# Changing banks between two halves of a matmul group: a drain of TensorE against a semaphore of its own matmuls

## The chip, the cores and the metric

One core of one Trainium2 chip runs one program. The metric is the device time of one execution in microseconds (us), 2326.66 before the change (median of 3 runs, 2324.75 to 2327.2).

## What is computed

The reference mixes two branches of the same input with a gate per token. One branch is softmax attention with 32 heads of width 18, the other a layer norm with a two-layer MLP (576 to 4608 to 576, GELU between). There are 2048 tokens.

```
x = A_x                                                   # [1, 2048, 576]
g = sigmoid((x * gate_w).sum(-1, keepdims=True))
q, k, v = (x @ wqkv) split into 32 heads of width 18
a = softmax(q @ k.T * 18 ** -0.5) @ v, heads joined, @ wo
h = gelu(layernorm(x) @ w1 + b1)                          # 4608 wide
b = h @ w2 + b2
out = g * a + (1 - g) * b
```

All in float32. A product that has to be exact is made of three matmuls in a faster rounded format: each operand is split into a high and a low part, and high x high, high x low and low x high are summed in PSUM.

## The kernel before, in words

A first part (to about 250 us) projects queries, keys and values. Then one long loop does the attention and the MLP together. Its order of instructions is written out by the program: no scheduler moves anything, so what stands first in an engine's queue runs first.

**The loop.** There are 32 units (a pair of heads and half of the queries) of 16 steps, 512 steps in all; a step takes one chunk of 128 keys. The kernel finds the maxima of the scores ahead of their use, since softmax needs them before the exponentials.

- A **round** (`s1_round`, lines 192 to 204; `next_round`, 307) belongs to a unit two ahead. It makes two matmuls (L202, one for each head of the pair; one sits on rows 0 to 63 of TensorE's array and the other on rows 64 to 127, so that they run side by side), each into its own bank of PSUM from the pool `ps_s1`, which has three. VectorE reduces each bank to its maxima (L204). There are 32 rounds to a unit, two to a step.
- The **scores** of the second pass (`s2`, 243) are two matmuls side by side again (L251) into one double bank `pss`. There is only one of these: ScalarE's exponential (L253) of the scores before must have emptied it.
- `pv` (257) multiplies the exponentials of two chunks with the values (L268).
- Between these the loop calls `fill` (1222), which takes the next piece of the MLP from a generator (`mlp`, 315): the first layer of a pair of hidden chunks (`h_pair`, 465, matmuls L489, GELU on ScalarE and GpSimd), or the second layer for 128 tokens (`out_pair`, 583).

In the loop (1260 to 1282) `next_round()` stands ahead of the scores of the first half of a step and ahead of or behind those of the second half. The round, the scores and a piece of the MLP follow each other so.

**`out_pair`.** This is where the change is. It sums four hidden chunks of 128 rows into 128 tokens x 576 outputs: two banks of 288 columns each. Each product contracts over only 64 rows, so two matmuls run side by side, one on the upper and one on the lower half of the array. Two matmuls that run at the same time must not write to one bank. So there are two **turns** (L598): in the first, rows 0 to 63 sum into bank 0 and rows 64 to 127 into bank 1; in the second it is the other way round (`nn = h ^ turn`). Each turn has 12 steps (`k`), of one pair of matmuls each. Between the turns the last matmuls on one half must have ended before the other half writes into their bank, and that is what L603 is for:

```
            for turn in range(2):
                if turn == 1 and bare:
                    add(ps, g == 0)
                    ps = [psum(free_pool()) for _ in range(2)]
                elif turn == 1:
                    nc.tensor.drain()
```

`drain` holds TensorE's sequencer until all matmuls before it have ended. (`bare` is the end of the loop, when no rounds are left: there the turns use different banks, and nothing waits.) After the second turn VectorE adds both banks to the accumulator in SBUF (L593).

A piece of the MLP ends where `k` is in `ends`, a set that depends on the place in the step. Where an `out_pair` begins in the first place it is {7, 15}: the first piece holds steps 0 to 6, the second 7 to 14 with the change of turns at 12 in it, the third the rest. Behind a piece come the round and the scores of the loop. So in the program before, the instructions on TensorE around a change of turns are: round, scores, five pairs of the first turn, drain, three pairs of the second turn, round, scores.

The lines that matter here are L202, L204, L251, L253, L593, L603 and L614 (the output matmuls) of the kernel before. In the changed kernel the output matmuls are L630.

Of the kernel before, what the change touches and what calls it, by code (L numbers as in the profile page):

```python
# [28 lines left out]
G = 4  # L29
NFC = F // P  # L30
NG = NFC // G
ND = 288
# [26 lines left out]
def gated_mix_kernel(ctx: ExitStack, tc: tile.TileContext, x, wqkv, wo, w1, b1, w2, b2, gate_w, out):  # L59
    nc = tc.nc  # L60
# [38 lines left out]
    def psum(pool):  # L99
        return pool.tile([P, TB], F32, name="ps")  # L100
# [18 lines left out]
    def defer(n, fn):  # L119
        later.append((slot[0] + n, fn))  # L120
# [49 lines left out]
    def load_q(u):  # L170
        pair, half = unit(u)
        qa = QA[u % 3]
        for h in range(2):
            d0 = (2 * pair + h) * DH
            for i, part in enumerate((0, 0, 1)):
                r = 64 * h + i * DH
                dma_r(nc.sync, qa[r:r + DH, :], qk_scr[part, d0:d0 + DH, half * HALF:(half + 1) * HALF])

    def load_k(pair, c0=0, c1=S):
        ka = KA[pair % 3]  # L180
        for h in range(2):
            d0 = D + (2 * pair + h) * DH
            for i, part in enumerate((0, 1, 0)):
                r = 64 * h + i * DH
                dma_r(nc.sync, ka[r:r + DH, c0:c1], qk_scr[part, d0:d0 + DH, c0:c1])
# [6 lines left out]
    def s1_round(u, r):  # L192


        t, kb = (r % 8, r // 8) if u == 0 else divmod(r, 4)
        if r == 0:
            M4[u] = asm.tile([P, 2, 8, 4], F32, name="m4")
        qa, ka = QA[u % 3], KA[UNITS[u][0] % 3]
        for h in range(2):
            r0 = 64 * h  # L200
            ps = psum(ps_s1)
            nc.tensor.matmul(ps, qa[r0:r0 + 54, t * P:(t + 1) * P], ka[r0:r0 + 54, kb * TB:(kb + 1) * TB],  # L202
                             start=True, stop=True)
            nc.vector.tensor_reduce(M4[u][:, h, t, kb:kb + 1], ps, axis=AX.X, op=ALU.max)  # L204

    def s1_finish(u):

        m4 = M4.pop(u)
        nm = asm.tile([P, 2, 8], F32, name="nm")
        nm2 = asm.tile([P, 2, 2, 8], F32, name="nm2")  # L210
        nmh = asm.tile([P, 2, 8], F32R, name="nmh")
        nc.vector.tensor_reduce(nm, m4, axis=AX.X, op=ALU.max, negate=True)
        nc.vector.tensor_copy(nmh, nm)
        nc.vector.tensor_copy(nm2[:, :, 0, :], nmh.bitcast(F32))
        nc.vector.tensor_tensor(nm2[:, :, 1, :], nm, nmh.bitcast(F32), op=ALU.subtract)

        def rows():
            ps = psum(ps_s1)
            nc.tensor.transpose(ps[:32, :P], nm2.rearrange("p a b c -> p (a b c)"), ident)
            mr = asm.tile([32, P], F32R, name="mr", bufs=1)  # L220
            nc.scalar.activation(mr, ps[:32, :P], AF.Copy)
            qa = QA[u % 3]
            aside = slot[0] < ybusy[0]

            def store(h, b):
                r = 64 * h + 54 + b
                k = (h * 2 + b) * 8
                dma_r(nc.scalar if aside else nc.sync,
                      qa[r:r + 1, :].rearrange("o (t n) -> o t n", n=P), mr[k:k + 8, :].bitcast(F32))
            for k in range(4):  # L230
                if aside:
                    defer(1 + 2 * k, lambda k=k: store(*divmod(k, 2)))
                else:
                    store(*divmod(k, 2))
        if looped[0]:
            ROWS.append(rows)
        else:
            defer(8, rows)
# [62 lines left out]
    rounds = [(u, r) for u in range(NU) for r in range(NR)]  # L301
# [5 lines left out]
    def next_round():  # L307
        if rounds:
            u, r = rounds.pop()
            s1_round(u, r)  # L310
            if r == NR - 1:
                defer(1, lambda: s1_finish(u))


    def mlp():
        W1, W2, HT = {}, {}, {}
        RAW = {}
# [88 lines left out]
        def ready(table, key):  # L406
            while key not in table:
                bg.pop(0)[1]()
            return table[key]
# [35 lines left out]
        def cuts(n, pieces):  # L445

            return {(k * n + pieces - 1) // pieces for k in range(1, pieces)}
# [3 lines left out]
        def free_pool():  # L451

            if rounds:
                return ps_w
            turns[0] += 1
            return (ps_s1, ps_w)[(turns[0] - 1) // 2 % 2]
# [126 lines left out]
        def out_pair(i, t, acc):  # L583

            tb, g = seq[i]
            tok = slice(t * P, (t + 1) * P)
            cs = [slice(nn * ND, (nn + 1) * ND) for nn in range(2)]
            bare = not rounds

            def add(ps, base):  # L590
                for nn in range(2):
                    dst = acc[:, t, cs[nn]]
                    nc.vector.scalar_tensor_tensor(dst, ps[nn][:, :ND], 0.5, b2b[:, cs[nn]] if base else dst,  # L593
                                                   op0=ALU.mult, op1=ALU.add)
            ps = [psum(free_pool()) for _ in range(2)]
            ends = {7, 15} if piece[0] == 0 else cuts(24, (3, 2, 1)[piece[0]])
            k = 0
            for turn in range(2):  # L598
                if turn == 1 and bare:
                    add(ps, g == 0)  # L600
                    ps = [psum(free_pool()) for _ in range(2)]
                elif turn == 1:
                    nc.tensor.drain()  # L603
                for j in ORDER:
                    while (i, j) not in HT:
                        cut[0] = 3
                        yield 0
                    hh, hl = HT[i, j]
                    w_ = ready(W2, (i * (G // 2) + j // 2, j % 2))
                    for h_, p_ in ((hh, 0), (hh, 1), (hl, 0)):  # L610
                        for h in (0, 1) if turn == 0 else (1, 0):
                            r = slice(64 * h, 64 * h + 64)
                            nn = h ^ turn
                            nc.tensor.matmul(ps[nn][:, :ND], h_[r, tok], w_[p_][r, cs[nn]],  # L614
                                             start=(k == 0 or bare and k == 3 * G), stop=(k == 6 * G - 1 or bare and k == 3 * G - 1))
                        k += 1
                        if k < 6 * G:
                            if k in ends:
                                cut[0] = 1
                            yield 131  # L620
            add(ps, g == 0 and not bare)
            if g == NG - 1:
                tt = TBS[tb] * 4 + t
                nc.gpsimd.tensor_scalar(acc[:, t, :], acc[:, t, :], gate1[:, tt:tt + 1], 1.0, op0=ALU.mult, op1=ALU.mult)
                defer(12 if tb < NB - 1 else 4, lambda: nc.sync.dma_start(b_scr[tt * P:(tt + 1) * P, :], acc[:, t, :]))
            cut[0] = 2
            yield 131
# [69 lines left out]
    made = []  # L697
    W = {}
    stream = [mlp()]
    spent = [0.0]  # L700
    cut = [0]
# [43 lines left out]
    with ExitStack() as a:  # L745
# [215 lines left out]
        for tb in range(NB):  # L961
# [3 lines left out]
            for g, (fn, args) in enumerate(work):  # L965
# [49 lines left out]
                if tb == 2 and g == 13:  # L1015
                    ps = psum(ps_s1)
# [18 lines left out]
    RING.append(ring2)  # L1035


    def out_proj():

        OT, BT, done, tmp = {}, {}, {}, {}  # L1040
# [123 lines left out]
        for b in range(NB):  # L1164
            per = 4 if b == 2 else 1
            res = {}
            for i0 in range(0, 8, per):
# [3 lines left out]
                ps = {}  # L1171
                for cut_ in (range(4), range(4, 5)):
                    for t, n in tiles:
                        tok = slice(t * P, (t + 1) * P)
                        cs = slice(n * ND, (n + 1) * ND)
# [3 lines left out]
                        for c in cut_:  # L1179
# [3 lines left out]
                            for k, (s_, w_) in enumerate(prods):  # L1183
                                nc.tensor.matmul(ps[t, n][:, :ND], OT[b][3][:, s_, tok], w_part(w_, c)[:, cs],  # L1184
                                                 start=(c == 0 and k == 0), stop=(c == 4 and k == 1))
# [60 lines left out]
    for u in range(NU):  # L1246
        for kc in range(NT):
            step = u * NT + kc
            if kc == 1:
                if u + 2 < NU:  # L1250
                    load_q(u + 2)
                if u % 2 == 0 and u // 2 + 1 < NPAIR - 1:
                    load_k(u // 2 + 1)
                    load_v(u // 2 + 1)
                elif u == NU - 5:
                    load_k(NPAIR - 1)
                elif u == NU - 4:
                    load_v(NPAIR - 1)
            at[0] = step

            next_round()
            s2(u, kc, 0)
            run_due(462.0)
            if kc % 2:
                fill(step, 1)
            elif step > 0:
                pv(step - 2)
                while ROWS:
                    ROWS.pop(0)()
                run_due(2080.0)  # L1270
                if step <= 2 * LEAD:
                    next_round()
            else:
                fill(step, 2)
            if kc % 2:
                next_round()
            s2(u, kc, 1)
            if kc % 2 == 0:

                next_round()  # L1280
            run_due(462.0)
            fill(step, 2 if kc % 2 else 0)
    pv(NSTEP - 2)
# [28 lines left out]
```

## Time and profile before

| | |
|---|---|
| median of 3 runs | 2326.66 us |
| the profiled execution | 2327.55 us |
| its span, first to last instruction | 2325.8 us |
| mean granted clock of TensorE | 0.997 |
| TensorE busy / weight loads / VectorE / ScalarE / GpSimd | 99% / 69% / 72% / 59% / 41% |
| output matmuls on L614, each | 6,912 in all, 293 to 300 ns |
| rounds: matmuls on L202 | 2,048, 410 ns each, two at a time |
| maxima on L204 | 2,048, 684 ns each |
| exponentials on L253 | 1,024, 1,026 ns each |

The profile has one row for each group of instructions or each stretch of time. PE is TensorE's matmuls, PEld its weight loads (each matmul here has its own, and it runs beside the matmul before), DVE is VectorE, ACT ScalarE, POOL GpSimd. A tile that is written stands left of the arrow, those that are read right of it. "64*128" means 64 rows and 128 columns of the array. "idle before" is the time in which the engine did nothing ahead of the instruction, and the name behind the arrow is what ended it; "issue" is idle time which ended with nothing that the profile shows. Matmuls are pipelined and their ends are modelled: a pair side by side shows as two overlapping rows, and two starts a little over 0.13 us apart are two pairs at full pace.

### The profile page before, as it was taken

To read this page: it belongs to the slowest core of one execution; us is meant where nothing else is said; L and a number is where in the kernel's file an instruction comes from. 1 tells how busy PE (TensorE), PEld (TensorE's weight loads), DVE (VectorE), ACT (ScalarE), POOL (GpSimd) and SP (SyncE) were. 2 spreads that over 40 slices of the span, in tenths; PEclk is the share of its full clock that TensorE was granted. 3 is DMA by queue.
4 is the path that set the end of the run, shared out by engine and by line. 5 is a ranking of instruction groups with operands and counts; after the bars stand their busy time and mean duration, and the time that the engine had idled before them with its cause. 6 is when DMAs were issued, how large, how long until landed. Compare 5 with 4: busy or idle time off the path is not lost.

```text
span 2325.8 us, 50689 instructions
## 1 busy us (share of the span) xinstructions
PE 2295.2 (99%) x20601; PEld 1615.4 (69%) x20601; DVE 1663.7 (72%) x2921; ACT 1379.9 (59%) x1631; POOL 947.8 (41%) x936
## 2 busy tenths in 40 slices
PE   8999999999999999999999999999999999999999
PEld 7878666666666666666666666666666666666669
DVE  5675777777777777777777777777777777777545
ACT  4223666666666666666666666666666666666662
POOL 4002466566553434443444344434434443333320
PEclk9999899999999999999999999999999999999999
DMA  7756545445473524232263324233364233322346
GB/s 242 247 190 197 175 144 170 157 136 169 139 187 131 164 86 127 96 118 96 90 174 144 114 94 134 81 118 116 118 162 153 94 118 107 106 97 101 113 139 223
DMA packets 160654, 323.58 MB, mean 139 GB/s; under 512 B 56062, under 2 KB 83618, under 8 KB 149586
## 3 DMA queue, kind: packets, MB, share of 16 engines
q1 hardware_dynamic: 156582, 313.57, 43.1%
q10 hardware_dynamic: 3840, 6.78, 0.8%
q8 instruction: 162, 2.65, 0.5%
q14 instruction: 70, 0.57, 0.1%
HBM read 229.07 MB, written 95.16 MB: 139 GB/s over the span
## 4 chain that ended last, share of the span: by engine, by line
PE 90%; POOL 3%; DVE 2%; issue 2%; DMA 1%; ACT 1%; SPq 0%; ACTq 0%; POOLq 0%; DVEq 0%
PE ps L614 20%; PE ps L268 19%; PE ps L489 17%; PE pss L251 12%; PE ps L202 11%; PE ps L880 4%; PE ps L1184 3%; PE ps L898 2%; POOL zz L159 1%; POOL w L159 1%; POOL hl L159 1%; DVE m L204 1%; DMA wraw<-in_B_w_dram 1%; PE ps L795 0%; DMA p<-in_A_wqkv_dram 0%
## 5 line engine op out<-in xcount | busy, mean ns | idle before, releaser
L204 DVE TENSOR_REDUCE m<-ps 128x1 f32<-128x512 f32 x2048 | 1297.3, 684 | 431.2 <-PE ps L202 429.7
L253 ACT ACTIVATE p<-pss 128x1024 f32<-128x1024 f32 x684 | 701.7, 1026 | 456.9 <-PE pss L251 445.3
L489 PE MATMUL ps<-big,w 64*128 64x512 f32 x3834 | 514.8, 392 | 0.1
L614 PE MATMUL ps<-w,hh 64*128 64x288 f32 x4352 | 501.2, 300 | 13.8 <-ACT z L512 2.1
L159 POOL TENSOR_SCALAR zz<-zz 128x512 f32<-128x512 f32 x272 | 169.3, 622 | 827.4 <-ACT zz L575 761.8
L251 PE MATMUL pss<-qa,ka 56*128 56x512 f32 x2048 | 484.1, 437 | 3.8 <-ACT p L253 1.1
L253 ACT ACTIVATE ring<-pss 128x1024 f32<-128x1024 f32 x340 | 348.9, 1026 | 231.4 <-PE pss L251 225.6
L202 PE MATMUL ps<-ka,qa 54*128 54x512 f32 x2048 | 460.8, 410 | 2.8 <-DVE m L204 1.2
L614 PEld LDWEIGHTS ps<-w,hh 64*128 64x128 f32 x4352 | 402.4, 186 | 68.9 <-issue 42.4
L489 PEld LDWEIGHTS ps<-big,w 64*128 64x128 f32 x3834 | 390.1, 185 | 59.6 <-ACT vt L909 0.3
L159 POOL TENSOR_TENSOR zz<-zz,z 128x512 f32<-128x512 f32 x280 | 361.4, 1291 | 35.6 <-ACT zz L577 10.5
L251 PEld LDWEIGHTS pss<-qa,ka 56*128 56x128 f32 x2048 | 198.0, 185 | 254.6 <-ACT p L253 121.4
L614 PE MATMUL ps<-w,hl 64*128 64x288 f32 x2176 | 351.7, 293 | 0.0
L268 PE MATMUL ps<-p,vt 128*32 128x512 f32 x2736 | 344.5, 598 | 0.0
L202 PEld LDWEIGHTS ps<-ka,qa 54*128 54x128 f32 x2048 | 244.5, 185 | 34.0 <-DVE m L204 12.1
L614 PEld LDWEIGHTS ps<-w,hl 64*128 64x128 f32 x2176 | 236.2, 186 | 0.5
L159 POOL TENSOR_TENSOR w<-x,w 128x576 fp32r<-128x576 f32 (+1 forms) x34 | 68.3, 2012 | 308.8 <-ACT w L385 304.6
L159 POOL TENSOR_TENSOR hl<-zz,hh 128x512 fp32r<-128x512 f32 x134 | 174.1, 1300 | 19.0 <-ACT hh L538 8.1
L268 PE MATMUL ps<-ring,vt 128*32 128x512 f32 x1360 | 179.1, 598 | 0.0
L268 PEld LDWEIGHTS ps<-p,vt 128*32 128x32 f32 x2736 | 71.4, 109 | 147.3 <-issue 147.3
L593 DVE SCALAR_TENSOR_TENSOR x<-ps,x 128x288 f32<-128x288 f32 x270 | 110.8, 452 | 29.8 <-PE ps L614 16.4
L880 PE MATMUL ps<-big,wqk 128*128 128x512 f32 x504 | 123.4, 399 | 0.1
(122 smaller groups left out, 1403.3 us busy)
## 6 DMA issues: line engine op xcount, KB each, us to landing
w<-w_scr SPq DMA_DIRECT2D x54, 1152.0 KB
w<-w_scr SPq DMA_DIRECT2D x108, 576.0 KB
w_scr<-w SPq DMA_DIRECT2D x18, 1152.0 KB
w_scr<-w SPq DMA_DIRECT2D x36, 576.0 KB
qa<-qk_scr SPq DMA_DIRECT2D x192, 72.0 KB
ka<-qk_scr SPq DMA_DIRECT2D x90, 144.0 KB
x<-in_B_w_dram SPq DMA_DIRECT2D x34, 288.0 KB
qk_scr<-hh SPq DMA_DIRECT2D x36, 256.0 KB
```

The lines of the kernel that those rows point to most:

```text
L159: fn(*args, **kw)
L202: nc.tensor.matmul(ps, qa[r0:r0 + 54, t * P:(t + 1) * P], ka[r0:r0 + 54, kb * TB:(kb + 1) * TB], start=True, stop=True)
L204: nc.vector.tensor_reduce(M4[u][:, h, t, kb:kb + 1], ps, axis=AX.X, op=ALU.max)
L251: nc.tensor.matmul(ps[:, h, :], ka[r0:r0 + 56, kc * P:(kc + 1) * P], qa[r0:r0 + 56, qb * TB:(qb + 1) * TB], start=True, stop=True)
L253: nc.scalar.activation(RING[n % 3][:, qb], ps, AF.Exp, scale=SCALE)
L268: nc.tensor.matmul(OB[u][r:r + 32, :], v[:, k, 19 * h:19 * h + 32], RING[c % 3][:, qb, h, :], start=(k == 0), stop=(k == NT - 1))
L489: nc.tensor.matmul(ps[h], wt[w_][r, c, :], Y[s_][r, c, :], start=(k == 0), stop=(k == 26))
L593: nc.vector.scalar_tensor_tensor(dst, ps[nn][:, :ND], 0.5, b2b[:, cs[nn]] if base else dst, op0=ALU.mult, op1=ALU.add)
L614: nc.tensor.matmul(ps[nn][:, :ND], h_[r, tok], w_[p_][r, cs[nn]], start=(k == 0 or bare and k == 3 * G), stop=(k == 6 * G - 1 or bare and ...
L880: nc.tensor.matmul(ps, w_[:, c, ms], big[:, s_, :], start=(k == 0), stop=(k == len(prods) - 1))
L898: nc.tensor.matmul(ps[:, :ND], big[:, s_, tok], w_[:, c, cs], start=(k == 0), stop=False)
L1184: nc.tensor.matmul(ps[t, n][:, :ND], OT[b][3][:, s_, tok], w_part(w_, c)[:, cs], start=(c == 0 and k == 0), stop=(c == 4 and k == 1))
```

## The change

The drain between the turns becomes a wait on a semaphore, `turn_sem`, which the last matmul of the first turn on each half raises by one when it ends. The first matmul of the second turn waits until it has risen by two more. Two calls tell the framework that this wait takes the place of its own tracking; they put no instruction anywhere.

In front of the wait the generator issues one round of maxima's scores (`lend_round`), if rounds are left and no piece ends just there. The loop leaves out the next round that it would have issued itself (`loop_round`), so that their number stays.

```
+    lent = [0]
+
+    def lend_round():
+        if rounds and not lent[0]:
+            next_round()
+            lent[0] = 1
+
+    def loop_round():
+        if lent[0]:
+            lent[0] = 0
+        else:
+            next_round()
...
                 elif turn == 1:
-                    nc.tensor.drain()
+                    if 3 * G not in ends:
+                        lend_round()
+                    turned[0] += 2
+                    nc.tensor.wait_ge(turn_sem, turned[0])
...
-                            nc.tensor.matmul(ps[nn][:, :ND], h_[r, tok], w_[p_][r, cs[nn]],
-                                             start=(k == 0 or bare and k == 3 * G), stop=(k == 6 * G - 1 or bare and k == 3 * G - 1))
+                            mm = nc.tensor.matmul(ps[nn][:, :ND], h_[r, tok], w_[p_][r, cs[nn]],
+                                                  start=(k == 0 or bare and k == 3 * G), stop=(k == 6 * G - 1 or bare and k == 3 * G - 1))
+                            if bare:
+                                continue
+                            if k == 3 * G - 1:
+                                mm.then_inc(turn_sem, 1)
+                                tc.no_tile_sem_insts.add(mm.ins.name)
+                                tc.add_to_no_dep_group(f"turn{turned[0]}", mm.ins)
+                            elif k == 3 * G and h == 0:
+                                tc.declare_fence(mm.ins, group=f"turn{turned[0] - 2}")
...
+    turn_sem = tc.alloc_semaphore("turn")
+    turned = [0]
...
-            next_round()
+            loop_round()
             s2(u, kc, 0)
...
             if kc % 2:
-                next_round()
+                loop_round()
             s2(u, kc, 1)
             if kc % 2 == 0:
 
-                next_round()
+                loop_round()
```

What this does to the order shows on TensorE. Here are its instructions around one change of turns in the middle of the loop (the weights' tiles w_12473, w_12471, w_12467 are the hidden chunks in the order in which a turn takes them; a turn ends with w_12471 and begins with w_12467; the drain itself is not among the rows). Before:

```order
L614 MATMUL ps<-w_12473,hl 128x288 x2
L614 MATMUL ps<-w_12471,hh 128x288 x4
L614 MATMUL ps<-w_12471,hl 128x288 x2
L614 MATMUL ps<-w_12467,hh 128x288 x4
L614 MATMUL ps<-w_12467,hl 128x288 x2
L202 MATMUL ps<-ka_106,qa_104 128x512 [waits DVE_49] x2
L251 MATMUL pss<-qa_105,ka_108 128x512 [waits Activation_49]
```

The second turn begins at the row of w_12467,hh, three pairs ahead of the round. The same place in the changed kernel:

```order
L630 MATMUL ps<-w_12473,hl 128x288 x2
L630 MATMUL ps<-w_12471,hh 128x288 x4
L630 MATMUL ps<-w_12471,hl 128x288 x2
L202 MATMUL ps<-ka_106,qa_104 128x512 [waits DVE_49] x2
L630 MATMUL ps<-w_12467,hh 128x288 [waits turn]
L630 MATMUL ps<-w_12467,hh 128x288 x3
L630 MATMUL ps<-w_12467,hl 128x288 x2
L251 MATMUL pss<-qa_105,ka_108 128x512 [waits Activation_49]
```

The round has moved up by three pairs, to between the turns, and the first matmul behind it waits for the new semaphore. This occurs at all 137 changes of turns that had a drain; the other 7 of the 144 are the bare ones. The order on VectorE, ScalarE, GpSimd and the DMA queues is the same as before.

## The prediction

> **What bounds the kernel now.** I read the page first (busy shares, chain), then the list of waits, then the line of the drain by itself, and last the timeline of one stretch of 6 us in which the place that the change touches occurs once. From the page, the busy shares and the chain by engine:
>
> ```profile
> PE 2295.2 (99%) x20601; PEld 1615.4 (69%) x20601; DVE 1663.7 (72%) x2921; ACT 1379.9 (59%) x1631; POOL 947.8 (41%) x936
> PEclk9999899999999999999999999999999999999999
> PE 90%; POOL 3%; DVE 2%; issue 2%; DMA 1%; ACT 1%; SPq 0%; ACTq 0%; POOLq 0%; DVEq 0%
> ```
>
> TensorE carries 90% of the chain, at the full granted clock. Its 99% busy is modelled, so small holes are not in it; they show as idle time of the weight loads (PEld). The drain's own row (count; least, median, greatest ns), and from the list of waits (total us, times, longest us):
>
> ```profile
> L603 PEldq DRAIN  x137: 875/1188/1912, 256.3 to 2191.0; - x137
> ...
> PEld pss L251 <- ACT p L253: 121.4, 229, 1.4
> PEld pss L251 <- ACT ring L253: 62.4, 117, 1.0
> PEld ps L614 <- issue: 42.4, 137, 0.4
> PEld ps L202 <- DVE m L204: 12.1, 26, 0.8
> ```
>
> There are 137 drains, and 137 times the weight load of an output matmul follows idle time that no other engine ended: 42.4 / 137 = 0.31 us each. The drain's 1.2 us is no measure of the cost: the loads idle for 0.31 of it, so the sequencer reaches it early, with matmuls still queued. The row of L251 on L253 matters later: scores of the second pass wait 346 times for the exponential that empties their only bank.
>
> Now one site (start, length, engine, line; x counts instructions merged):
>
> ```profile
> 1013.54 0.19 PEld L251 LDWEIGHTS pss<-qa,ka 56*128 56x128 f32 x2 [0.84 <-ACT p L253]
> 1014.14 1.03 ACT L253 ACTIVATE p<-pss 128x1024 f32<-128x1024 f32 x1 [1.26 <-PE pss L251]
> 1014.30 2.48 DVE L204 TENSOR_REDUCE m<-ps 128x1 f32<-128x512 f32 x4 [0.99 <-PE ps L202]
> 1014.37 0.29 PE L614 MATMUL ps<-w,hl 64*128 64x288 f32 x2
> 1014.51 0.42 PE L614 MATMUL ps<-w,hh 64*128 64x288 f32 x4
> 1014.77 0.29 PE L614 MATMUL ps<-w,hl 64*128 64x288 f32 x2
> 1015.87 1.03 ACT L253 ACTIVATE ring<-pss 128x1024 f32<-128x1024 f32 x1 [0.71 <-PE pss L251]
> 1016.09 0.35 PE L614 MATMUL ps<-w,hl 64*128 64x288 f32 x2
> 1016.51 0.30 PEld L614 LDWEIGHTS ps<-w,hh 64*128 64x128 f32 x4 [0.31 <-issue]
> 1016.52 0.53 PE L614 MATMUL ps<-w,hh 64*128 64x288 f32 x4
> 1016.88 0.29 PE L614 MATMUL ps<-w,hl 64*128 64x288 f32 x2
> 1017.02 0.40 PE L202 MATMUL ps<-ka,qa 54*128 54x512 f32 x2
> 1017.25 0.40 PE L251 MATMUL pss<-qa,ka 56*128 56x512 f32 x2
> 1017.78 1.03 ACT L253 ACTIVATE ring<-pss 128x1024 f32<-128x1024 f32 x1 [0.88 <-PE pss L251]
> 1018.55 0.30 PE L614 MATMUL ps<-w,hl 64*128 64x288 f32 x2
> 1018.68 0.41 PE L202 MATMUL ps<-ka,qa 54*128 54x512 f32 x2
> 1018.86 0.26 PEld L251 LDWEIGHTS pss<-qa,ka 56*128 56x128 f32 x2
> 1018.87 0.82 DVE L593 SCALAR_TENSOR_TENSOR x<-ps,x 128x288 f32<-128x288 f32 x2
> 1018.92 0.51 PE L251 MATMUL pss<-qa,ka 56*128 56x512 f32 x2
> 1019.53 1.02 ACT L253 ACTIVATE p<-pss 128x1024 f32<-128x1024 f32 x1 [0.72 <-PE pss L251]
> ```
>
> The pair at 1016.09 is the last before the change of banks, the load at 1016.51 the first behind the drain. The round of maxima's scores that the change moves stands at 1017.02; the s2 scores at 1017.25 follow it.
>
> **1. The drain goes.** From the end of the pair before it (1016.09 + 0.35 = 1016.44) to the end of the third pair behind it (1016.88 + 0.29 = 1017.17) it takes 0.73 us; the same three pairs without a stop, from the pair at 1014.37 to that at 1014.77, take 0.40. The stop costs 0.33 us a site, near the 0.31 of the list, and 137 x 0.33 = 45 us over the run. All of it is on TensorE's path.
>
> **2. The wait comes.** No row shows TensorE waiting for itself, so I put it together. VectorE, waiting for the last output pair (1018.55, ending 1018.85), starts its add at 1018.87: 0.02 us behind the modelled end, its own start included. TensorE, waiting for ScalarE's exponential (1017.78 + 1.03 = 1018.81), starts its weight load at 1018.86: 0.05 behind. Together 0.05 to 0.07: the first load of the second turn would start at 1016.49 to 1016.51, where it starts now. So the wait **alone** gains 0 to 0.02 us a site, next to nothing: it lasts as long as the drain, since both wait for the same two matmuls. From above I bound it by a wait that ends only when the lent round has ended too: that round starts 0.13 behind the pair at 1016.09 (pairs follow so at 1014.37 and 1014.51), at 1016.22, ends by the model 0.40 later at 1016.62, and a load 0.07 behind that is 0.18 later than now. I take the lower end, since the load at 1018.86 starts while the round of 1018.68 is still in flight: a wait in front of a load does not wait for other matmuls. Queued behind the waiting load are all of TensorE's later instructions, hence also ScalarE's next exponential and VectorE's next maxima.
>
> **3. The round moves up by three pairs of matmuls, into the hole.** It takes TensorE 0.23 to 0.24 us where it stands (1017.02 to 1017.25, 1018.68 to 1018.92). In the new place it runs from 1016.22 to 1016.45 and the array waits for the load at 1016.49 to 1016.51 anyway, so it costs nothing there. Its cover is the stop; without that it would cost the same 0.23. The order of instructions has 137 such moves, none by more than three pairs, and one round less at the next regular place each time. TensorE's own gain: 0.23 for the round and 0 to 0.02 for the wait, 0.24 a site, 137 x 0.24 = 33 us.
>
> **4. What the round needs.** A bank out of three, which VectorE empties. VectorE's four reductions from 1014.30 take 0.62 each; the moved round's first matmul needs the second (1015.54, long done), its second matmul the third, done at 1016.16. With 0.05 to the load it loads at 1016.21 rather than at once, and ends about 0.1 + 0.23 later, at 1016.54. The first matmul of the second turn on that half of the rows starts 0.1 behind its load (the 0.53 of the four at 1016.52 against 0.42 of the four at 1014.51), at 1016.60. So this wait is hidden too, by about 0.06 us. VectorE gets the round's scores 0.80 us earlier (1016.22 for 1017.02); its order does not change, nor that of ScalarE, GpSimd or the queues.
>
> **5. What is late next: ScalarE.** By TensorE alone the s2 scores would start at 1017.25 - 0.24 = 1017.01. They need the bank that the exponential of 1015.87 leaves at 1016.90. Today the next exponential starts 0.88 behind that. How short can this be? In the two places where the load waited for the exponential, it starts 0.05 behind (1018.81 to 1018.86), and the next exponential 0.60 (1013.54 to 1014.14) to 0.67 (1018.86 to 1019.53) behind the load: 0.65 to 0.72 in all. So the exponential can move up by 0.16 to 0.23, and not by 0.24: ScalarE takes back 0.01 to 0.08 of TensorE's gain. A site with another spacing agrees:
>
> ```profile
> 1399.02 1.03 ACT L253 ACTIVATE p<-pss 128x1024 f32<-128x1024 f32 x1 [0.72 <-PE pss L251]
> 1399.23 0.41 PE L614 MATMUL ps<-w,hl 64*128 64x288 f32 x2
> 1399.72 0.30 PEld L614 LDWEIGHTS ps<-w,hh 64*128 64x128 f32 x4 [0.31 <-issue]
> 1400.46 0.40 PE L251 MATMUL pss<-qa,ka 56*128 56x512 f32 x2
> 1400.90 1.03 ACT L253 ACTIVATE p<-pss 128x1024 f32<-128x1024 f32 x1 [0.34 <-PE pss L251]
> ```
>
> There the exponential ends at 1400.05 and the next starts 0.85 behind: room for 0.13 to 0.20. Over both sites 0.13 to 0.23; I take 0.20, since the loads at a site follow a fresh start of both halves, as the one with 0.60 does. Everything later in the cycle (the waiting s2 load of 1018.86 too) hangs on this exponential and moves with it.
>
> **The sum.** 137 x 0.20 = 27 us (18 to 32 by the ends). The profiled execution took 2327.55 us, its span of 2325.8 and 1.75 around it; it lies 0.9 us above the median of the runs, 2326.66. From the median: 2299.5. Measurement can tell about 0.2%, 4.7 us, from no change.
>
> **The rivals.**
> *ScalarE does not hold it back* (0.11): where the later s2 scores have slack, TensorE's 0.24 counts in full: 33 us, 2293.5. For it: only 346 of the loads for 684 + 340 exponentials are listed as waiting.
>
> ```profile
> L253 ACT ACTIVATE p<-pss 128x1024 f32<-128x1024 f32 x684 | 701.7, 1026 | 456.9 <-PE pss L251 445.3
> L253 ACT ACTIVATE ring<-pss 128x1024 f32<-128x1024 f32 x340 | 348.9, 1026 | 231.4 <-PE pss L251 225.6
> ```
>
> Against: the two sites above.
> *The wait ends later than the drain did* (0.15). Both matmuls of the last pair raise the semaphore, and if these steps come one behind the other the release comes late; the longest idle time in the row of L614 is 0.4 against 0.31 on average, 0.09 more. TensorE's gain is then 0.15 a site, 20 us, 2306; by the upper bound of part 2, 0.24 - 0.18 = 0.06, 8 us, 2318.5. Against it: the add at 1018.87, 0.02 us behind its pair. On this the Trainium skill, "TensorE: Matmul & The Clock Gate", section "The cost: per-tile semaphore tail", says that increments on the matmuls of several tiles serialise, and that one on the last matmul would do: about 25 + 4.7 ns a tile + 26.3 ns an increment, by which I estimate 87 ns for two tiles and two increments against the 0.02 of the row. By that figure the load starts 0.07 later, TensorE gains 0.17, and the sum is 23 us, 2303.5.
> *No change* (0.07): the exponentials alone set the pace, and what the site gains the next s2 wait takes. For it: 121.4 + 62.4 us of such waits. Against: at the sites the exponential starts 0.85 to 0.88 behind the last, where 0.65 to 0.72 is possible.
> *Slower* (0.05): the moved round's second matmul meets a bank that VectorE has not emptied, and all of TensorE stands behind it. It is covered for 0.06 us (part 4); beyond that each late microsecond is lost whole, and from 0.26 us late the site is slower than now. A single add ahead of the third reduction would do it:
>
> ```profile
> L593 DVE SCALAR_TENSOR_TENSOR x<-ps,x 128x288 f32<-128x288 f32 x270 | 110.8, 452 | 29.8 <-PE ps L614 16.4
> ```
>
> At 0.45 us it would cost 0.19 a site, 26 us, 2352.5. Against: VectorE's four reductions there follow each other without an add, and its order stays.
>
> That the change does not take place is no rival: the drains are gone from the program and the rounds stand in the new places.
>
> **The numbers.** The forecast has 0.62: 2295 to 2308.5 by its ends. The range reaches to the first rival (2293.5, and 2 us for a wait that ends sooner) and through most of the second: 2291 to 2313. Outside lie the late end of the second, no change and slower: under 0.2. Faster by over 0.2%: 0.62 + 0.11 + 0.15 = 0.88; within it 0.07; slower 0.05.
>
> **What would show it.** Right: no DRAIN row; the row of idle weight loads behind the change of banks falls from 0.31 to under 0.15 each, as the round's loads stand in it; from the start of the last pair of the first turn to the first load of the second still 0.40 to 0.44 us; the exponentials around a site 1.7 us apart rather than 1.91 (1015.87 to 1017.78); TensorE's waits for L253 more often, 0.05 us each; the stretch from 1013.54, one cycle of two steps, 0.2 us shorter. Wrong: a first load of the second turn that starts 0.48 us or more behind the last pair's start (second rival), waits of L202 on L204 well over 26 times with 0.2 us or more each (slower), or cycles as long as before with longer waits on L253 (no change).

## The result and the profile after

| | us |
|---|---|
| before, median of 4 runs (2324.75 to 2327.2) | 2326.65 |
| changed kernel, median of 4 runs (2296.81 to 2299.79) | 2298.19 |
| ratio, with its 95% interval | 0.9878 (0.9863 to 0.9893) |
| profiled execution of the changed kernel / its span | 2296.81 / 2295.0 |

The change saves 28.5 us, 0.208 us for each of the 137 changes of banks. From the page of the changed kernel, the busy shares, the granted clock and the chain by engine:

```profile
PE 2273.5 (99%) x20601; PEld 1620.6 (71%) x20601; DVE 1654.4 (72%) x2921; ACT 1379.2 (60%) x1631; POOL 946.6 (41%) x936
PEclk9999999999999999999999999999999999999999
PE 90%; POOL 4%; DVE 2%; ACT 2%; DMA 1%; issue 1%; SPq 0%; ACTq 0%; POOLq 0%; DVEq 0%
```

VectorE, ScalarE and GpSimd are busy for as long as before, to within 10 us; TensorE's modelled busy time is 22 us less. TensorE keeps 90% of the chain, and no other share moves by more than a point. From the list of waits of the changed kernel, and the weight-load group of the output matmuls that holds the first load of each turn, before (L614) and after (L630; behind the second bar stands the idle time before them):

```profile
PEld pss L251 <- ACT p L253: 120.5, 218, 1.4
PEld pss L251 <- ACT ring L253: 61.7, 110, 1.0
PEld ps L202 <- DVE m L204: 12.1, 25, 0.8
...
L614 PEld LDWEIGHTS ps<-w,hh 64*128 64x128 f32 x4352 | 402.4, 186 | 68.9 <-issue 42.4
...
L630 PEld LDWEIGHTS ps<-w,hh 64*128 64x128 f32 x4352 | 397.9, 186 | 32.2 <-ACT z L525 2.5
```

The row of 137 waits of output loads is gone from the list, and the idle time before that group fell from 68.9 to 32.2 us, by 0.27 a place. L202 waits for L204 no more than before (25 times, 12.1 us). Now the place in the loop that the prediction worked with, the same instructions in the changed kernel:

```profile
1002.67 1.03 ACT L253 ACTIVATE ring<-pss 128x1024 f32<-128x1024 f32 x1 [0.71 <-PE pss L251]
...
1002.89 0.35 PE L630 MATMUL ps<-w,hl 64*128 64x288 f32 x2
1002.89 0.34 PEld L202 LDWEIGHTS ps<-ka,qa 54*128 54x128 f32 x2
1003.02 0.52 PE L202 MATMUL ps<-ka,qa 54*128 54x512 f32 x2
1003.29 0.30 PEld L630 LDWEIGHTS ps<-w,hh 64*128 64x128 f32 x4
1003.30 0.54 PE L630 MATMUL ps<-w,hh 64*128 64x288 f32 x4
1003.54 0.19 PEld L630 LDWEIGHTS ps<-w,hl 64*128 64x128 f32 x2
1003.67 0.30 PE L630 MATMUL ps<-w,hl 64*128 64x288 f32 x2
1003.75 0.19 PEld L251 LDWEIGHTS pss<-qa,ka 56*128 56x128 f32 x2
1003.80 0.46 PE L251 MATMUL pss<-qa,ka 56*128 56x512 f32 x2
...
1004.38 1.03 ACT L253 ACTIVATE ring<-pss 128x1024 f32<-128x1024 f32 x1 [0.68 <-PE pss L251]
```

The last pair of the first turn starts at 1002.89, the lent round 0.13 behind it, and the first load of the second turn at 1003.29: 0.40 behind the pair, where it was 0.42 with the drain. The second half of the round was held for about 0.1 (a load row of 0.34 rather than 0.19): in the trace its load starts at 1003.04, 0.05 behind the end of the reduction that empties its bank. It did not delay the first load of the second turn. The s2 load at 1003.75 starts 0.05 behind the exponential's end (1002.67 + 1.03 = 1003.70): **it is ScalarE that it waits for**. The start of the s2 matmul does not show this, for it follows the third pair by 0.13, as at full pace; what comes late is its load, only 0.05 ahead of it, and with the load the scores: the exponential starts 0.58 behind the s2 matmul's start, where it was 0.53 (1017.25 to 1017.78). From the last exponential's end it is 0.68, where it was 0.88.

To see where the time went I took the start of every exponential less the start of the one before, in both traces, and subtracted. The 137 intervals that hold a change of banks give 29.2 us of the 30.8 by which the two spans differ; the interval before, and the three behind, give 0.3 to 0.6 us each. So nothing was handed back later in the cycle.

### The profile page after: what moved, and what is told of

Read it like the earlier page. It is cut to its first block, busy times and chain, and to the rows that moved or that the text cites. A ratio compares the mean times of both kernels' runs of the same rounds, so it can differ in the third digit from the quotient of the medians.

```text
span 2295.0 us, 50552 instructions
## 1 busy us (share of the span) xinstructions
PE 2273.5 (99%) x20601; PEld 1620.6 (71%) x20601; DVE 1654.4 (72%) x2921; ACT 1379.2 (60%) x1631; POOL 946.6 (41%) x936
## 4 chain that ended last, share of the span: by engine, by line
PE 90%; POOL 4%; DVE 2%; ACT 2%; DMA 1%; issue 1%; SPq 0%; ACTq 0%; POOLq 0%; DVEq 0%
PE ps L268 19%; PE ps L630 19%; PE ps L502 17%; PE pss L251 13%; PE ps L202 11%; PE ps L904 5%; PE ps L1211 2%; PE ps L922 2%; POOL zz L159 1%; POOL w L159 1%; POOL hl L159 1%; DVE m L204 1%; PE ps L819 1%; DMA wraw<-in_B_w_dram 1%; ACT p L253 0%
## 5 line engine op out<-in xcount | busy, mean ns | idle before, releaser
L204 DVE TENSOR_REDUCE m<-ps 128x1 f32<-128x512 f32 x2048 | 1284.8, 683 | 341.8 <-PE ps L202 339.1
L253 ACT ACTIVATE p<-pss 128x1024 f32<-128x1024 f32 x684 | 701.1, 1025 | 436.6 <-PE pss L251 422.5
L630 PE MATMUL ps<-w,hh 64*128 64x288 f32 x4352 | 498.2, 297 | 2.8 <-ACT z L525 2.1
L202 PE MATMUL ps<-ka,qa 54*128 54x512 f32 x2048 | 479.9, 413 | 3.1 <-DVE m L204 1.7
L253 ACT ACTIVATE ring<-pss 128x1024 f32<-128x1024 f32 x340 | 348.6, 1025 | 221.1 <-PE pss L251 213.6
L630 PEld LDWEIGHTS ps<-w,hh 64*128 64x128 f32 x4352 | 397.9, 186 | 32.2 <-ACT z L525 2.5
L630 PE MATMUL ps<-w,hl 64*128 64x288 f32 x2176 | 348.9, 292 | 0.0
L202 PEld LDWEIGHTS ps<-ka,qa 54*128 54x128 f32 x2048 | 265.4, 185 | 34.8 <-DVE m L204 12.1
L630 PEld LDWEIGHTS ps<-w,hl 64*128 64x128 f32 x2176 | 233.2, 186 | 0.4
L159 POOL TENSOR_TENSOR hl<-zz,hh 128x512 fp32r<-128x512 f32 x134 | 174.1, 1300 | 17.2 <-DMA vt<-v_scr 4.3
```

Of the source, the lines that this page charges most:

```text
L159: fn(*args, **kw)
L253: nc.scalar.activation(RING[n % 3][:, qb], ps, AF.Exp, scale=SCALE)
L630: mm = nc.tensor.matmul(ps[nn][:, :ND], h_[r, tok], w_[p_][r, cs[nn]], start=(k == 0 or bare and k == 3 * G), stop=(k == 6 * G - 1 or bare ...
```

## The experiments

**The two parts apart.** First the semaphore without the lent round:

```
                 elif turn == 1:
-                    if 3 * G not in ends:
-                        lend_round()
                     turned[0] += 2
                     nc.tensor.wait_ge(turn_sem, turned[0])
```

> The changed kernel without the lent round: semaphore in place of the drain, the round where it stood before. My theory: the semaphore and the drain wait for the same two matmuls, so the first load of the second turn starts 0.35 us behind the last matmul instead of 0.37; 137 x 0.00 to 0.02 us = 0 to 3 us faster than before, and 25 us or more slower than the changed kernel. Rival (the drain itself is dear, for the sequencer has to come to rest): most of the gain is here already, 15 to 28 us faster than before.

Measured: 2323.42 us against 2326.77, ratio 0.9989 (0.9980 to 0.9997), 3.3 us faster and 25 us slower than the changed kernel. In its trace, from the list of waits and the timeline:

```profile
PEld ps L628 <- PE ps L628: 40.0, 137, 0.4
...
1013.91 0.36 PE L628 MATMUL ps<-w,hl 64*128 64x288 f32 x2
1014.33 0.30 PEld L628 LDWEIGHTS ps<-w,hh 64*128 64x128 f32 x4 [0.29 <-PE ps L628]
```

The 137 waits are all there, 0.29 us each, and now the profile can name what ended them, TensorE's own L628. The load stands 0.42 behind the pair's start in this view; over all places its distance from the last single matmul is 0.347 us as a median, against 0.365 with the drain. The semaphore releases 0.018 us earlier. The drain's price is the wait for the matmuls, and a semaphore pays the same.

Then the lent round with the drain behind it:

```
                     if 3 * G not in ends:
                         lend_round()
-                    turned[0] += 2
-                    nc.tensor.wait_ge(turn_sem, turned[0])
+                    nc.tensor.drain()
```

> The changed kernel with the drain back in its place, behind the lent round. My theory: the drain waits for the round's matmuls too, of which the second ends about 0.60 us behind the last output matmul (load held by VectorE's bank until 0.10, 0.1 to the matmul, 0.21 of columns, 0.19 until it is through); the first load of the second turn starts at 0.66 instead of 0.37 without the round. The round saves 0.23 elsewhere: 0.06 us lost a site, 137 x 0.06 = 8 us slower than before, at most as fast as before. Rival (any work in the hole fills it, whatever the wait): about as fast as the changed kernel, 25 to 28 us faster than before.

Measured: 2336.06 us, ratio 1.0041 (1.0028 to 1.0054), 9.3 us slower than before. The rows of the place, behind that of the list of waits:

```profile
PEld ps L629 <- issue: 57.0, 137, 0.6
...
1017.37 0.36 PE L629 MATMUL ps<-w,hl 64*128 64x288 f32 x2
1017.37 0.34 PEld L202 LDWEIGHTS ps<-ka,qa 54*128 54x128 f32 x2
1017.50 0.54 PE L202 MATMUL ps<-ka,qa 54*128 54x512 f32 x2
1018.13 0.30 PEld L629 LDWEIGHTS ps<-w,hh 64*128 64x128 f32 x4 [0.42 <-issue]
```

With the drain the load comes 0.76 behind the pair, not 0.40: it waits for the round too (its matmuls end by the model at 1018.04). The round fills a hole and makes a new one behind it, of 57.0 / 137 = 0.42 us, longer than the old. Neither part gives the gain by itself (3.3 us from the one, a loss of 9.3 from the other); what gains the 28 us is a wait **for two named matmuls** with other work behind them.

**Is it ScalarE that takes back the rest?** The exponential of the scores was cut into two halves, each with a bank of PSUM of its own, in the kernel before and in the changed one (the pool now has two single banks for its one double bank, and the matmuls write to `ps[h]`):

```
-        ps = ps_s2.tile([P, 2, TB], F32, name="pss")
+        ps = [psum(ps_s2) for _ in range(2)]
...
-        nc.scalar.activation(RING[n % 3][:, qb], ps, AF.Exp, scale=SCALE)
+        for h in range(2):
+            nc.scalar.activation(RING[n % 3][:, qb, h], ps[h], AF.Exp, scale=SCALE)
```

> The kernel before, with the exponential of the scores in two halves of 512 columns, each with a bank of its own, so that the next scores' first matmul waits for the first half alone. My theory: scores that wait for ScalarE now (541 of 1,023 loads start 0.05 us behind the end of an exponential) come earlier, at up to 0.1 us each: 20 to 50 us faster than before, less what the longer busy time of ScalarE costs (two halves of about 0.62 against 1.03). The rival (ScalarE sets no pace) expects no gain, or a loss.

> The changed kernel with the exponential in two halves in the same way. My theory: ScalarE took back 0.03 to 0.04 us of TensorE's 0.24 at each of the 137 places; with it out of the way the change is worth the full 0.24: this kernel is about 33 us (31 to 35) faster than the kernel before with the split exponential, where the changed kernel is 28 us faster than the one before. Rival (the site gains 0.20 for another reason, as a wait that ends later than I think): the difference stays at 28 us or below.

Measured: 2314.24 us for the first (ratio 0.9948, 0.9935 to 0.9960) and 2281.45 us for the second (0.9806, 0.9793 to 0.9819). The first gained 12.5 us, less than the 20 to 50 expected. The difference of the two is 32.8 us, as the theory had it (33, 31 to 35). With ScalarE out of the way each place is worth 32.8 / 137 = 0.24 us, and by the exponentials' intervals all of it arises at the 137 places (34.4 us there, where the two profiled spans differ by 32.2). The exponentials of the second kernel as groups, and one place of it in the timeline:

```profile
L254 ACT ACTIVATE p<-ps 128x512 f32<-128x512 f32 x1368 | 742.7, 595 | 384.5 <-PE ps L251 376.4 <-PE ps L202 2.2
...
996.63 1.09 ACT L254 ACTIVATE ring<-ps 128x512 f32<-128x512 f32 x2 [0.55 <-PE ps L251]
996.97 0.40 PE L630 MATMUL ps<-w,hl 64*128 64x288 f32 x2
997.79 0.29 PE L630 MATMUL ps<-w,hl 64*128 64x288 f32 x2
997.79 0.19 PEld L251 LDWEIGHTS ps<-qa,ka 56*128 56x128 f32 x2
997.92 0.40 PE L251 MATMUL ps<-qa,ka 56*128 56x512 f32 x2
```

The load of the scores behind the change of banks now starts with the third pair of the second turn (997.79), 0.13 ahead of its matmul, where ScalarE let it start only 0.05 ahead in the changed kernel. At all 137 places it starts 0.38 us or more behind the end of the first half's exponential: the bank was free before. This kernel is 45 us faster than the one before.

**The rival that would have made it slower.** The lent round's second matmul needs a bank from VectorE, which was free with 0.06 us to spare by my working. An extra operation on VectorE ahead of that reduction, in both kernels, takes this cover away:

```
                         if k < 6 * G:
+                            if k == 7 and not bare:
+                                nc.vector.scalar_tensor_tensor(junk2, b2b[:, :ND], 0.5, b2b[:, ND:], op0=ALU.mult, op1=ALU.add)
                             if k in ends:
```

> The kernel before, with one more operation on VectorE at each place: 288 columns out of SBUF and back, about 0.45 us, behind the seventh pair of the first turn, so that it stands ahead of the two reductions that come before the drain (and one buffer fewer for the results at the very end). Its result is not used. My theory: VectorE idles there for 0.67 us before the next round's maxima, and the banks that the next round needs are free before it comes: within 3 us of the kernel before. The rival (VectorE has no room here) expects 20 us or more slower.

> The changed kernel with the same extra operation on VectorE. My theory: the lent round's second matmul needs the bank that the first of these two reductions empties, 0.45 us later now; it was covered for 0.06 us, so 0.39 is lost and the 0.24 of TensorE's gain becomes a loss of 0.15 a place: 137 x 0.15 = 20 us slower than the kernel before with the extra operation (10 to 30). Rival (the hole behind the first turn covers VectorE too): still 25 us or more faster than that one.

Measured: 2336.58 us for the first (ratio 1.0047, 1.0031 to 1.0064) and 2357.02 us for the second (1.0126, 1.0111 to 1.0142). The second is 20.4 us slower than the first: with a busier VectorE the same change loses, as the rival said, and the sum is the expected one. From the lists of waits of the first and the second kernel, and the place in the second:

```profile
PEld ps L202 <- DVE m L204: 16.1, 35, 0.8
...
PEld ps L202 <- DVE m L204: 79.0, 161, 1.4
...
1025.37 0.45 DVE L643 SCALAR_TENSOR_TENSOR junk<-b2b 128x288 f32<-128x288 f32 x1
...
1025.74 2.48 DVE L204 TENSOR_REDUCE m<-ps 128x1 f32<-128x512 f32 x4
...
1025.95 0.35 PE L630 MATMUL ps<-w,hl 64*128 64x288 f32 x2
1025.96 0.18 PEld L202 LDWEIGHTS ps<-ka,qa 54*128 54x128 f32 x1
1026.09 0.88 PE L202 MATMUL ps<-ka,qa 54*128 54x512 f32 x2
1026.47 0.18 PEld L202 LDWEIGHTS ps<-ka,qa 54*128 54x128 f32 x1 [0.33 <-DVE m L204]
1026.48 0.29 PEld L630 LDWEIGHTS ps<-w,hh 64*128 64x128 f32 x3
```

The round's loads wait for VectorE's bank 161 times, not 35. At the place shown the four reductions start at 1025.74, of 0.68 us each; the first ends at 1026.42, the round's second load starts 0.05 behind, at 1026.47, and the loads of the second turn follow it at once. The stall has moved from the semaphore to VectorE's bank, and it is longer.

Two things went otherwise than expected. The first kernel was to stay within 3 us and lost 10. By the exponentials' intervals 108 of its 137 places did not change, and the other 29 lost 9.7 us, 0.33 each. At 24 of these 29 the extra operation (L619) took 0.96 us or more, not 0.45; what the other five lost by is open. One of the 24, where VectorE copies an attention output a little earlier:

```profile
837.55 0.69 DVE L280 COPY oe<-ps 128x512 f32<-128x512 f32 x1 [0.41 <-PE ps L268]
...
839.40 0.98 DVE L619 SCALAR_TENSOR_TENSOR junk<-b2b 128x288 f32<-128x288 f32 x1
```

And the 20 us are not 0.15 at each place. The second kernel lost 0.07 at 97 places (6.4 us), where the extra operation took its usual 0.45 us but for two; it lost 0.32 at 36 places (11.6 us), and at each of these the operation took 0.51 us or more; at four it gained 1.7 us in all. That makes 16.3 of the 17.2 us between the two profiled spans. So that the sum agrees with the forecast is luck: the usual place lost half of what was expected, and operations longer than 0.45 us made up the rest. The direction and the bank that does it are shown.

**One increment or two.** On the kernel with the split exponential, where ScalarE hides nothing at these places:

```
-                                mm.then_inc(turn_sem, 1)
+                                if h == 1:
+                                    mm.then_inc(turn_sem, 1)
```

(with `turned[0] += 1` and the group's number to match)

> The changed kernel with the exponential in two halves, where only the very last matmul of the first turn raises the semaphore, by one, instead of the last on each half. My theory: the release follows the end of the last matmul by some hundredths of a us either way, the first load of the second turn stays 0.35 us behind it, and the time is that of the kernel with two increments within 2 us. The rule of the Trainium skill (TensorE: Matmul & The Clock Gate, section The cost: per-tile semaphore tail) would have 26 ns less a place, by which I estimate 137 x 0.026 = 3.6 us faster, with the load 0.32 us behind.

Measured: 2280.00 us, ratio 0.9798 (0.9784 to 0.9813), against 0.9806 (0.9793 to 0.9819) with two: no difference that these runs can tell. The first load stands 0.347 us behind the last matmul's start, as a median over all places, in both traces. The release comes 0.014 us behind the matmul's modelled end in both. The Trainium skill ("TensorE: Matmul & The Clock Gate", "The cost: per-tile semaphore tail") gives 26 ns an increment, since increments serialize. These two runs do not test that: with two increments the last two matmuls start 0.10 us or more apart at every place here, and the increments come 0.094 us or more apart, so neither waits for the other. The changed kernel's trace bears on it at four places, where the two matmuls start less than 0.03 apart: there the increments come 0.034 to 0.035 apart, and the release 0.021 to 0.048 behind the modelled end, against 0.013 to 0.015 at the other 133. That agrees with increments that serialize, and it is too rare here to cost anything.

## Why the prediction was right

The forecast was 2299.5 by 27 us of gain, 0.20 a place; measured were 28.5 us and 0.208.

- **Part 1, the stop.** 0.33 us from one place; as a mean over all 137 the second pair of the second turn starts 0.346 later than at full pace. Right.
- **Part 2, the wait alone.** 0 to 0.02 us a place; the experiment gave 3.3 us / 137 = 0.024, and the trace 0.018 by the position of the load. Right. The taken end, that a wait ahead of a load does not wait for the round in flight, is what sets the changed kernel (0.40) apart from the one with drain and round (0.76).
- **Part 3, the round in the hole.** TensorE's own gain was put at 0.24 a place; with the exponential split it is 32.8 / 137 = 0.24. Right.
- **Part 4, the bank.** The hidden wait is there: at 131 of the 137 places the round's second load starts 0.05 us behind the end of a reduction, and it costs nothing that shows. With VectorE later it costs, as the rival said. The size of the cover was not right. The third reduction ends at 1016.19, not at 1016.16 (each takes 0.68, and they start 0.60 apart), which by the same working leaves 0.03 and not 0.06. The experiment says more: the reduction was 0.37 late (1025.74 rather than 1025.37), and the usual place went from 0.20 gained to 0.07 lost, 0.27, so that by this estimate about 0.1 was covered. Why it is more than the rows give was not tried.
- **Part 5, ScalarE.** From the end of one exponential to the start of the next I expected 0.65 to 0.72 at the least; over the 137 places the median is 0.654 (0.860 before), and 677 of the 1,023 s2 loads start within 0.06 us of an exponential's end, where 541 did. Of the 137 loads at the places it is 136, where it was one. The split exponential shows it by time. I took 0.20 from the middle of the bounds; by the median it was 0.206.
- **What would show it.** Of the signs of being right, the first load of the second turn stands at 0.40, as asked; the exponentials around the place are 1.71 us apart; the idle time before that load is 0.08 a place, under 0.15; and a cycle of two steps takes 7.49 us (1000.33 to 1007.82) rather than 7.67. One sign was chosen badly: I expected the list of waits to show L253 more often. It shows 218 and 110 waits instead of 229 and 117, since it leaves out short idle times, and there are only 0.02 us between the end of the load before and this load. The waits are counted in the timeline's distances, as above.

The rival that ScalarE would not hold TensorE back fell with the split exponential: 33 us come only when it is out of the way. The rival of a later release fell with the traces: the load stands 0.40 behind the pair and not 0.48, and the release is late at four places alone. The exponentials' pace (no change) is a bound in this kernel, but one with 0.20 us of room at these places; the room is now used up.

## What to carry to other kernels

A drain and a semaphore on the last matmul cost nearly the same (0.018 us apart here) when nothing stands between the matmul and the wait; the gain of a semaphore is that independent work can stand there without being waited for. Choose that work by what it needs: here a round fitted because its bank came free some hundredths of a microsecond earlier, and the same edit lost 20 us when VectorE was a little later. When a hole on the busiest engine is closed, look for the loop of the next one (here score, exponential, bank, 1.03 + 0.65 us) and work out how much of the gain it lets through before counting the rest.

## What the runs showed of the hardware that was not expected

- Two exponentials of 512 columns cost ScalarE hardly more than one of 1,024: 595 ns each as single rows, but back to back they overlap, 1.09 us for the two against 1.03 for the one. ScalarE's busy time rose from 1379.9 to 1437.2 us only.
- The extra VectorE operation, with the same operands each time, took 446 to 450 ns at the 55 places where GpSimd was idle (in the kernel before with the extra operation), and a median of 545, up to 1,489 ns, at the 81 where GpSimd was busy for more than half of it. What makes it slower was not tried.
- When one half of the array is held (the round's second matmul at 1026.47), the other half runs ahead with the next pairs: its first two matmuls of the second turn start at 1026.48 and 1026.72, those of the held half at 1026.81 and 1026.94. Whether this is why 97 of 137 places lost only 0.07 us where 0.15 was expected is not shown.
